# Zero fills on ScalarE, earlier second-tile scores and an earlier w_out load at the start of a fused attention and MLP kernel

## The chip, the cores and the metric

The kernel runs on one core of a Trainium2 chip. The metric is the device time of one execution in microseconds (us); lower is better. TensorE (PE in the profile) multiplies matrices, VectorE (DVE), ScalarE (ACT) and GpSimd (POOL) work element by element, SyncE (SP) issues transfers. GpSimd issues transfers too. All transfers run on the same 16 DMA engines.

## What is computed

Forgetting attention on 8 batches of 8 heads, 576 positions and head size 64, followed by a two-layer MLP with a tanh GELU on the 4608 resulting rows:

```python
scores = scale * q @ k.T                       # per batch and head, 576 x 576
cum    = cumsum(log(clip(f, 1e-4, 1)))         # forget gates
scores = where(causal, -1e9, scores + cum_i - cum_j)
attn   = softmax(scores);  x = attn @ v        # x: 4608 x 512
h      = x @ w_in                              # 512 x 2048
out    = gelu_tanh(h) @ w_out                  # 2048 x 512
```

The kernel never forms the decay matrix. It folds exp(-cum - 64) into the values (tile `vw`) and into a vector `w_bf` that gives the denominators, so that scores only need an exponential and the causal mask.

## The kernel before

**Tiling.** Heads are taken four at a time: 16 quads, two to a batch. A quad's q and k (`q_c`, `k_c`) are loaded with a cast to bf16, and VectorE transposes them into `qT`, `kT` (L197). Scores go to PSUM tiles `ps_s`, of which there are two, each for two heads; ScalarE takes their exponential into `pt` (L268), GpSimd masks the diagonal blocks (L274), TensorE multiplies with `w_bf` for denominators and with `vw` for values (L314 for the first two quads, L328 later), and VectorE normalizes into `xT` (L359). Rows of `xT` are then the input of the MLP, which works on chunks of 512 rows: w_in products (L490 for the first chunk, L373 and L432 later), GELU on ScalarE into `gT`, w_out products (L610 for chunk 0, L540 later).

**Order.** Nothing is scheduled automatically. The whole order is written out as words in tables (`SETUP`, `FRONT` and one table for each later chunk), and `run` issues them one after another; each engine executes its own instructions strictly in that order. The words that matter here:

- `TK.i`, `TQ.i`: transposes of k and q of quad i. `S.i.r`: scores of quad i, part r, with their exponentials; `H.i.r.g` the same for heads 2g and 2g+1 only. For the first two quads, part 0 is the first 256 query rows, parts 1 to 3 the rest.
- `M.i.r`: masks on GpSimd. `D.i.p`: denominators; `V.i.x.p`: values; p is the half (first 256 rows or the rest).
- `CU`, `CW`: the two products that sum the logarithms (L669, L673); `CW` also computes `wT` on ScalarE (L675). `W`: casts of `wT` to `w_bf` on VectorE. `vw`, `VW`: weighted values on VectorE or GpSimd (L214).
- `B.n.c`: n filler matmuls of c columns whose result nobody reads (L239).
- `LP.t`: load of tile t of v of batch 0. `WI.c`, `WO.c`: loads of pieces of w_in (L180, six pieces) and w_out (L184, four pieces), `LQ`, `LK`: of q and k. All of these are issued from GpSimd's queue, in line with its masks. `X@Y` makes the issue of X wait until load Y has landed (`LU.t` is the load `LP.t`).
- `J`, `j`: steps of the first chunk's w_in products for half of its rows (L490). `F.0.n`: n steps of the output product of chunk 0 (L610), sixteen to a block of 128 rows.

A load that GpSimd issues takes one of eight semaphores in turn, so it also waits for the load eight places before it.

**The start.** `setup` issues the loads of f, q and k, clears the tiles whose unused parts are read (on VectorE, L629 to L641), clamps f (L642), takes its logarithm on ScalarE (L643) and transposes it (L648, copied back at L650 and L651). Tile `v_nat` has rows past the 576th position, `vw` a spare slot `LOW`, and `w_bf` the same slot; these are the zero parts that the change touches (L637 to L641).

Of the kernel before, what the change touches and what calls it, by code (L numbers as in the profile page):

```python
# [16 lines left out]
def kernel(  # L17
# [10 lines left out]
    nc = tc.nc  # L28

    B, H, S, D = q.shape  # L30
    BH = B * H
# [35 lines left out]
    LOW, HIGH = NT, NT - 1  # L67

    SETUP = """
        TK.0 LP.0 LP.1  # L70
    """

    FRONT = """
        TQ.0 B.2.256 TR TK.1 SB B.2.128 CU S.0.0 CW B.5.384 B.1.256 TQ.1 W WI.0 WI.1 vw.0.0 LP.2@LQ.0 M.0.0 LP.4 S.0.2 B.3.384 H.1.0.1 H.1.0.0
        vw.1.0 LP.3 WI.2@LU.1 M.1.0.1 D.0.0 M.1.0.0 WI.3 WI.4 WI.5 H.1.1.1 V.0.0.0 H.0.1.1 V.0.1.0 D.1.0 H.0.1.0 V.1.0.0 M.0.1 LQ.2 LK.2 H.1.1.0
        M.1.1 V.1.1.0 H.0.3.0 j.0.0 H.0.3.1 j.0.0 M.0.3 H.1.3.0 j.0.0 vw.0.1 H.1.3.1 j.0.0 M.1.3 VW.1.1 H.1.2.0 D.0.1 H.1.2.1 j.0.0 J.0.1 V.0.1.1
        V.0.0.1 D.1.1 J.0.2 WO.0 WO.1@LU.4 V.1.1.1 V.1.0.1 J.0.3 J.1.0 WO.2@WI.5 WO.3 J.1.1 TQ.2 LK.3 LQ.3 J.1.2 J.1.3 LX.1.0@WO.0 LQ.4 TK.2 X F.0.6
        LK.4 TK.3 S.2.0 M.2.0 LK.5 F.0.9 S.2.2 M.2.2 LX.1.1@WO.2 F.0.10 S.2.1 TQ.3 TQ.4 F.0.10 LV.2.0@LK.5 m.2.1 vw.2 TK.4 S.3.0 f.0.1 CL.2 LQ.5
        VW.3 D.2 f.0.6 S.3.1 m.3.0 F.0.6 V.2.0 S.3.2 TK.5 LK.6 M.3.2 f.0.7 V.2.1 CL.3 S.4.1 m.3.1 LQ.6 F.0.6 TQ.5 H.4.2.1 D.3 H.4.0.1 LQ.7 VW.4
        H.4.0.0 V.3.1 v.3.0 f.0.3 H.4.2.0 CL.4 I.1.0 m.4.1 U.0 LV.2.1@LQ.5 I.1.4 TQ.6 m.4.2.3 I.1.1 I.1.5 U.1 LV.3.0@LQ.7 LV.3.1 m.4.2.2 TK.6 G.0  # L80
        M.4.0 LK.7 LQ.8 LK.8 I.1.2 I.1.3 U.3 K.1.0 K.1.1 K.1.2 I.1.6 I.1.7 G.1.1.2 U.2 X F.1.16 S.5.0 f.1.26 S.5.1 D.4 M.5.0 f.1.16 S.5.2 V.4.0
        m.5.2.3 f.1.10 VW.5 V.4.1 K.1.3 CL.5 m.5.2.2 S.6.0 f.1.10 M.5.1 D.5 f.1.7 S.6.1 V.5.1 f.1.12 V.5.0 T.2 S.6.2 vw.6
    """

    HOMES = {1: 0, 3: 1, 0: 2}
# [41 lines left out]
    def many(n, shape, dtype, name):  # L127
        return [singles.tile(shape, dtype, name=f"{name}{i}") for i in range(n)]
# [6 lines left out]
    v_nat = many(2, [128, NT, H, D], FP32, "v_nat")  # L135
# [3 lines left out]
    vw = many(2, [128, NT + 1, 4, D], BF16, "vw")  # L139
# [10 lines left out]
    w_bf = singles.tile([128, NQ, NT + 1, 4], BF16, name="w_bf")  # L150
# [3 lines left out]
    idle = u4.rearrange("p t n -> p (t n)")[:, 0:512]  # L154
# [34 lines left out]
    def load_one(src, dst, i):  # L189
        b, h0 = i // QPB, 4 * (i % QPB)  # L190
        return nc.gpsimd.dma_start(
            out=dst[i % 2].rearrange("p a d -> p (a d)"),
            in_=src[b, h0:h0 + 4].rearrange("h (p a) d -> (h p) (a d)", p=32))
# [426 lines left out]
    def setup():  # L620
        nc.sync.dma_start(out=f_sb, in_=f.rearrange("b h s -> (b h) s"))
        dmas["LK.0"] = load_one(k, k_c, 0)
        dmas["LQ.0"] = load_one(q, q_c, 0)
        make_identity(nc, ident_f32)
        dmas["LK.1"] = load_one(k, k_c, 1)
        dmas["LQ.1"] = load_one(q, q_c, 1)
        make_upper_triangular(nc, utri_f32, val=1.0, diag=True)

        nc.vector.memset(idle, 0.0)  # L629
        nc.vector.memset(ones_f32, 1.0)  # L630
        nc.vector.memset(logfT, 0.0)
        nc.vector.memset(shift, -64.0)
        nc.vector.memset(wT[64:128, :, HIGH, :], 0.0)
        for t_ in kT:
            nc.vector.memset(t_[:, 0:64], 0.0)
            nc.vector.memset(t_[:, 64 + S:], 0.0)
        for t_ in v_nat:  # L637
            nc.vector.memset(t_[64:128, HIGH, :, :], 0.0)
        for t_ in vw:
            nc.vector.memset(t_[0:64, LOW, :, :], 0.0)  # L640
        nc.vector.memset(w_bf[0:64, :, LOW, :], 0.0)  # L641
        nc.vector.tensor_scalar(f_sb, f_sb, 1e-4, 1.0, op0=ALU.max, op1=ALU.min)  # L642
        nc.scalar.activation(f_sb, f_sb, AF.Ln)  # L643
        idle_ps.append(psO.tile([128, 1024], FP32, name="idle_ps", tag="po"))
        ps_lt = psM.tile([128, NT * BH], FP32, name="ps_lt", tag="m")
        for t in range(NT):
            n = min(128, S - 128 * t)
            nc.tensor.transpose(ps_lt[:n, t * BH:(t + 1) * BH], f_sb[:, 128 * t:128 * t + n], ident_f32)  # L648
        run(SETUP)
        nc.scalar.copy(logfT[:, :HIGH * BH], ps_lt[:, :HIGH * BH])  # L650
        nc.scalar.copy(logfT[0:64, HIGH * BH:], ps_lt[0:64, HIGH * BH:])  # L651

    def triangles(copy):
        for m in causal:
            copy(m, utri_f32)
        copy(causal[1][64:128, 0:64], utri_f32[0:64, 0:64])
# [37 lines left out]
    def cast_w(copy):  # L694
        copy(w_bf[:, :, 0:NT, :], wT)
        copy(w_bf[64:128, :, LOW, :], wT[0:64, :, 0, :])

    def load_values(b, half):
# [2 lines left out]
    ops = {  # L701
        "W": lambda: cast_w(nc.vector.tensor_copy),
        "w": lambda: cast_w(nc.scalar.copy),
        "CU": within_tiles,
        "CW": make_w,
        "SB": lambda: sums_before(nc.gpsimd),
# [38 lines left out]
    def run(table):  # L745

        for word in table.split():
            word, _, gate = word.partition("@")
            name, *args = word.split(".")
            did = ops[name](*map(int, args))  # L750
            did = did if isinstance(did, list) else [did]
            if gate:
                after(did[0], dmas[gate])
            dmas[word.replace("LP", "LU").replace("LX", "LV")] = did[-1]
# [31 lines left out]
    with tc.manual_schedule():  # L786
        setup()
        run(FRONT)
        for c in range(2, NCH):
            play(c)  # L790
        out_part(NCH - 1, CH)
# [30 lines left out]
```

## Time and profile before

| | |
|---|---|
| time, median of 3 runs | 324.67 us (323.61 to 325.16) |
| the profiled execution | 325.03 us, of which the span from first to last instruction is 323.3 us |
| TensorE busy | 310.7 us, 96% of the span |
| VectorE, ScalarE, GpSimd busy | 251.3, 206.9 and 111.4 us |
| chain that ended last | TensorE 89%, DMA 5%, ScalarE 2% |
| of the DMA part, loads of w_in | 3.5% of the span; of q, 1.7% |
| loads of w_in | six, issued from 8.0 to 18.7 us |
| loads of w_out | four, issued from 26.2 to 31.2 us |

How to read it: a busy share is an average over the whole span. The chain is followed back from the last instruction, each step to what released it. Where a step of the chain is a transfer or an engine other than TensorE, TensorE stood still or ran fillers. Idle time of other engines costs nothing in itself.

### The profile page before, as it was taken

How to read it: one execution, taken by the hardware profiler on the slowest of the kernel's cores; microseconds unless marked ns; L12 is line 12 of the kernel's file. 1: busy time of each engine (PE TensorE's matmuls, PEld its weight loads, DVE VectorE, ACT ScalarE, POOL GpSimd, SP SyncE). 2: the span in 40 equal slices, each digit the busy share in tenths (PEclk: the TensorE clock that was granted, in tenths of full speed). 3: DMA queues.
4: the chain of work that ended last, by engine and by line, in shares of the span. 5: the costliest groups of instructions: out<-in, count | busy, mean ns of one | idle time of the engine just before them, and what ended most of it. 6: DMA issues, size and time to landing. Idle time of an engine off the chain costs nothing.

```text
span 323.3 us, 12322 instructions
## 1 busy us (share of the span) xinstructions
PE 310.7 (96%) x5512; PEld 218.4 (68%) x5532; DVE 251.3 (78%) x401; ACT 206.9 (64%) x259; POOL 111.4 (34%) x158
## 2 busy tenths in 40 slices
PE   3898999999999999999999999999999999999995
PEld 1456844544777567776777687667766788788784
DVE  5754338897679899868986898689877969886882
ACT  4696486776757677568657784778666843732830
POOL 8786446650220116700681048303820150000000
PEclk9999999999999999999999999999999999999999
DMA  7999998889302931493129711981120012013013
GB/s 122 235 137 201 208 213 204 173 162 214 93 4 67 183 70 39 97 213 86 36 70 175 152 36 40 171 187 39 34 69 0 14 33 92 1 34 100 0 33 99
DMA packets 47029, 33.45 MB, mean 103 GB/s; under 512 B 29824, under 2 KB 41216, under 8 KB 46976
## 3 DMA queue, kind: packets, MB, share of 16 engines
q0 software_dynamic: 9168, 15.99, 29.0%
q1 hardware_dynamic: 37664, 16.60, 19.5%
q8 instruction: 43, 0.70, 1.0%
q14 instruction: 10, 0.08, 0.1%
q10 hardware_dynamic: 144, 0.07, 0.1%
HBM read 36.85 MB, written 9.44 MB: 143 GB/s over the span
## 4 chain that ended last, share of the span: by engine, by line
PE 89%; DMA 5%; ACT 2%; issue 1%; POOL 1%; DVE 1%; DVEq 0%; POOLq 0%
PE ps_w L540 30%; PE ps_h L373 16%; PE po L328 10%; PE ps_cd L432 8%; PE ps_s L260 8%; PE ps_ab L432 6%; DMA w_in_sb<-in_moe_w_in_dram 3%; PE pso L610 3%; PE ps_h L490 3%; PE ps_h L387 2%; DMA q_c<-in_q_dram 2%; ACT pt L268 1%; PE idle_ps L239 1%; PE ps_o L328 0%; POOL w_in_sb L180 0%
## 5 line engine op out<-in xcount | busy, mean ns | idle before, releaser
L268 ACT ACTIVATE pt<-ps_s 128x1024 bf16<-128x1024 f32 (+2 forms) x100 | 94.0, 988 | 39.0 <-PE ps_s L260 35.2
L274 POOL TENSOR_SCALAR_AFFINE_SELECT pt<-pt 128x512 bf16<-128x512 bf16 (+2 forms) x67 | 39.9, 605 | 107.7 <-ACT pt L268 106.6
L373 PE MATMUL ps_h<-xT,w_in_sb 128*128 128x512 bf16 x228 | 54.5, 379 | 0.6
L540 PEld LDWEIGHTS <-gT 128*32 128x32 bf16 (+1 forms) x1247 | 50.7, 97 | 6.0 <-issue 1.7
L540 PE MATMUL ps_w<-w_out_sb,gT 128*32 128x256 bf16 (+1 forms) x1050 | 47.0, 273 | 0.0
L380 ACT ACTIVATE gT<-ps_h 128x1024 bf16<-128x1024 f32 x30 | 30.6, 1020 | 17.2 <-PE ps_h L373 16.7
L540 PEld LDWEIGHTS <-gsum 128*32 128x32 bf16 (+1 forms) x1256 | 39.3, 97 | 1.4
L373 PEld LDWEIGHTS <-w_in_sb 128*128 128x128 bf16 x240 | 23.4, 98 | 24.3 <-issue 0.4
L260 PE MATMUL ps_s<-qT,kT 32*128 32x64 bf16 (+5 forms) x896 | 37.0, 264 | 1.4 <-DVE qT L197 0.9
L214 POOL TENSOR_TENSOR vw<-v_nat,wT 128x1280 bf16<-128x1280 f32 (+1 forms) x13 | 29.8, 2290 | 4.7 <-DMA v_nat<-in_v_dram 4.3
L540 PE MATMUL ps_w<-usum,gsum 128*32 128x256 bf16 (+1 forms) x832 | 30.6, 273 | 0.0
L260 PEld LDWEIGHTS <-kT 32*128 32x128 bf16 x896 | 16.8, 93 | 19.2 <-issue 13.6
L197 DVE STREAM_TRANSPOSE kT<-k_c 128x576 f32<-128x576 f32 x16 | 19.9, 1243 | 11.1 <-DMA k_c<-in_k_dram 11.1
L441 ACT ACTIVATE gT<-snap 128x512 bf16<-128x512 f32 x45 | 26.1, 625 | 3.0 <-DVE snap L455 2.4
L565 DVE TENSOR_TENSOR o_st<-ps_w,snap 128x512 f32<-128x512 f32 x31 | 21.2, 685 | 8.4 <-PE ps_w L540 7.2
L432 PEld LDWEIGHTS <-w_in_sb 128*128 128x128 bf16 x240 | 23.4, 98 | 6.2 <-issue 1.5
L328 PE MATMUL po<-pt,vw 128*32 128x64 bf16 (+4 forms) x624 | 22.5, 278 | 0.0
L359 DVE TENSOR_TENSOR xT<-po,rb 128x576 bf16<-128x576 f32 x26 | 19.5, 750 | 3.7 <-PE po L328 3.1
L328 PEld LDWEIGHTS <-vw 128*32 128x32 bf16 x672 | 14.5, 97 | 10.2 <-issue 3.7
L432 PEld LDWEIGHTS <-xT 128*128 128x128 bf16 x180 | 17.6, 98 | 5.2
L197 DVE STREAM_TRANSPOSE qT<-q_c 128x576 f32<-128x576 f32 x16 | 19.9, 1244 | 1.1 <-PE ps_s L260 0.7
L432 PE MATMUL ps_cd<-xT 128*128 128x256 bf16 x120 | 18.0, 273 | 0.0
(105 smaller groups left out, 464.9 us busy)
## 6 DMA issues: line engine op xcount, KB each, us to landing
out_dram<-o_st SPq DMA_DIRECT2D x35, 256.0 KB, 2.4
k_c<-in_k_dram POOLq DMA_DIRECT2D x16, 288.0 KB, 5.9
q_c<-in_q_dram POOLq DMA_DIRECT2D x16, 288.0 KB, 6.4
v_nat<-in_v_dram SPq DMA_DIRECT2D x16, 256.0 KB, 6.8
v_nat<-in_v_dram SPq DMA_DIRECT2D x20, 128.0 KB, 5.7
w_out_sb<-in_moe_w_out_dram POOLq DMA_DIRECT2D x4, 512.0 KB, 10.3
v_nat<-in_v_dram POOLq DMA_DIRECT2D x9, 128.0 KB, 5.5
v_nat<-in_v_dram POOLq DMA_DIRECT2D x4, 256.0 KB, 7.5
```

Source lines behind the costliest of these rows:

```text
L197: nc.vector.transpose(out=dst.rearrange("p s c -> p (s c)").bitcast(FP32) .rearrange("p (t a) -> p a t", a=S // 32), in_=src.rearrange("p ...
L214: eng.tensor_mul(vw[i % 2][:, t0:t1], vb[:, t0:t1, h0:h0 + 4, :], wT[:, i, t0:t1, :].unsqueeze(3).to_broadcast([128, t1 - t0, 4, D]))
L260: nc.tensor.matmul(tiles[h // 2][:, h % 2, c0:c0 + nq], key_columns(i, key, h, c), qq[32 * h:32 * h + 32, q0:q0 + nq, c], start=(c == 0 an ...
L268: nc.scalar.activation(p[:, 2 * g:2 * g + 2, off:off + n], t[:, :, 0:n], AF.Exp, scale=scale)
L274: nc.gpsimd.affine_select(out=x, in_=x, compare_op=ALU.is_ge, fill=0.0, base=0, pattern=pattern, channel_multiplier=-1)
L328: nc.tensor.matmul(po[r0:r0 + w.shape[-1], 448 + q0:448 + q0 + nq], w, p[:, h, col:col + nq], start=(key in (0, "low")), stop=(key in ("lo ...
L373: nc.tensor.matmul(ph[:, j, :], w_in_sb[:, dt, 128 * ft:128 * ft + 128], xT[:, dt, CH * c:CH * (c + 1)], start=(dt == 0), stop=(dt == N_DT ...
L380: nc.scalar.activation(gT[:, 2 * pr:2 * pr + 2, :], ph, AF.Gelu_apprx_tanh)
L432: nc.tensor.matmul(ps[:, j], w[:, dt, 128 * j:128 * j + 128], x[:, dt], start=(first and j == 0 and dt == 0), stop=(dt == 1), skip_group_c ...
L441: nc.scalar.activation(gT[:, ft:ft + 2, HC * j:HC * (j + 1)], x, AF.Gelu_apprx_tanh)
L540: nc.tensor.matmul(ps[c0:c0 + width, n, cols[0]:cols[1]], x[:, j, 128 * n + c0:128 * n + c0 + width], w[:, j, cols[0]:cols[1]], start=(fir ...
L565: nc.vector.tensor_add(st, ps, kept[name])
```

## The change

Three things, all in the first 55 us or so. First, the zero fills of `w_bf`, `vw` and `v_nat` leave VectorE and become copies on ScalarE from a tile of zeros (`idle`, which the first memset clears); the two of `vw` stand before the copies of the transposed logarithm, the other three after them. Second, the scores of part 2 of quad 0 come in two halves directly after `CW`, where six fillers stood; three fillers of 256 columns follow them, and three of 384 columns that followed `S.0.2` are dropped. Third, `LP.3` and `WI.2` stand ahead of the scores of quad 1, `WI.2` and `WO.1` no longer name a load to wait for, `WO.0` stands ahead of `M.1.3`. Beside these `D.0.0` moves behind the last w_in issues, `H.0.1.0` ahead of `D.1.0`, and of two words of chunk 0's output product, `F.0.9` and `F.0.10`, the longer one now comes first.

The core of the diff; in the table lines that are left out the words are the same:

```diff
     SETUP = """
-        TK.0 LP.0 LP.1
+        Z.1.2 TK.0 LP.0 LP.1
     """
     FRONT = """
-        TQ.0 B.2.256 TR TK.1 SB B.2.128 CU S.0.0 CW B.5.384 B.1.256 TQ.1 W WI.0 WI.1 vw.0.0 LP.2@LQ.0 M.0.0 LP.4 S.0.2 B.3.384 H.1.0.1 H.1.0.0
-        vw.1.0 LP.3 WI.2@LU.1 M.1.0.1 D.0.0 M.1.0.0 WI.3 WI.4 WI.5 H.1.1.1 V.0.0.0 H.0.1.1 V.0.1.0 D.1.0 H.0.1.0 V.1.0.0 M.0.1 LQ.2 LK.2 H.1.1.0
-        M.1.1 V.1.1.0 H.0.3.0 j.0.0 H.0.3.1 j.0.0 M.0.3 H.1.3.0 j.0.0 vw.0.1 H.1.3.1 j.0.0 M.1.3 VW.1.1 H.1.2.0 D.0.1 H.1.2.1 j.0.0 J.0.1 V.0.1.1
-        V.0.0.1 D.1.1 J.0.2 WO.0 WO.1@LU.4 V.1.1.1 V.1.0.1 J.0.3 J.1.0 WO.2@WI.5 WO.3 J.1.1 TQ.2 LK.3 LQ.3 J.1.2 J.1.3 LX.1.0@WO.0 LQ.4 TK.2 X F.0.6
-        LK.4 TK.3 S.2.0 M.2.0 LK.5 F.0.9 S.2.2 M.2.2 LX.1.1@WO.2 F.0.10 S.2.1 TQ.3 TQ.4 F.0.10 LV.2.0@LK.5 m.2.1 vw.2 TK.4 S.3.0 f.0.1 CL.2 LQ.5
+        TQ.0 B.2.256 TR TK.1 SB Z.0.3.4 B.2.128 CU S.0.0 CW H.0.2.0 H.0.2.1 B.3.256 TQ.1 W WI.0 WI.1 vw.0.0 LP.2@LQ.0 M.0.0 LP.4 LP.3 WI.2 H.1.0.1
+        H.1.0.0 vw.1.0 M.1.0.1 M.1.0.0 WI.3 WI.4 WI.5 D.0.0 H.1.1.1 V.0.0.0 H.0.1.1 V.0.1.0 H.0.1.0 D.1.0 V.1.0.0 M.0.1 LQ.2 LK.2 H.1.1.0 M.1.1
+        V.1.1.0 H.0.3.0 j.0.0 H.0.3.1 j.0.0 M.0.3 H.1.3.0 j.0.0 vw.0.1 H.1.3.1 j.0.0 WO.0 M.1.3 VW.1.1 H.1.2.0 D.0.1 H.1.2.1 j.0.0 J.0.1 V.0.1.1
+        V.0.0.1 D.1.1 J.0.2 WO.1 V.1.1.1 V.1.0.1 J.0.3 J.1.0 WO.2@WI.5 WO.3 J.1.1 TQ.2 LK.3 LQ.3 J.1.2 J.1.3 LX.1.0@WO.0 LQ.4 TK.2 X F.0.6 LK.4 TK.3
+        S.2.0 M.2.0 LK.5 F.0.10 S.2.2 M.2.2 LX.1.1@WO.2 F.0.9 S.2.1 TQ.3 TQ.4 F.0.10 LV.2.0@LK.5 m.2.1 vw.2 TK.4 S.3.0 f.0.1 CL.2 LQ.5 VW.3 D.2
...
     """
...
-        for t_ in v_nat:
-            nc.vector.memset(t_[64:128, HIGH, :, :], 0.0)
-        for t_ in vw:
-            nc.vector.memset(t_[0:64, LOW, :, :], 0.0)
-        nc.vector.memset(w_bf[0:64, :, LOW, :], 0.0)
...
+    def zeros(which):
+
+        todo = [(w_bf[0:64, :, LOW, :], idle[0:64, 0:BH].rearrange("p (i h) -> p i h", h=4))]
+        todo += [(t_[0:64, LOW, :, :], idle[0:64, 0:256].rearrange("p (h d) -> p h d", h=4)) for t_ in vw]
+        todo += [(t_[64:128, HIGH, :, :], idle[64:128, 0:512].rearrange("p (h d) -> p h d", h=H)) for t_ in v_nat]
+        for n in which:
+            nc.scalar.copy(*todo[n])
...
+        "Z": lambda *which: zeros(which),
```

`Z.1.2` clears the two `vw` tiles, `Z.0.3.4` clears `w_bf` and the two `v_nat` tiles.

More of the change, by code (lines that the diff above doesn't have):

```diff
@@ L77 @@
-        V.0.0.1 D.1.1 J.0.2 WO.0 WO.1@LU.4 V.1.1.1 V.1.0.1 J.0.3 J.1.0 WO.2@WI.5 WO.3 J.1.1 TQ.2 LK.3 LQ.3 J.1.2 J.1.3 LX.1.0@WO.0 LQ.4 TK.2 X F.0.6
-        LK.4 TK.3 S.2.0 M.2.0 LK.5 F.0.9 S.2.2 M.2.2 LX.1.1@WO.2 F.0.10 S.2.1 TQ.3 TQ.4 F.0.10 LV.2.0@LK.5 m.2.1 vw.2 TK.4 S.3.0 f.0.1 CL.2 LQ.5
-        VW.3 D.2 f.0.6 S.3.1 m.3.0 F.0.6 V.2.0 S.3.2 TK.5 LK.6 M.3.2 f.0.7 V.2.1 CL.3 S.4.1 m.3.1 LQ.6 F.0.6 TQ.5 H.4.2.1 D.3 H.4.0.1 LQ.7 VW.4
-        H.4.0.0 V.3.1 v.3.0 f.0.3 H.4.2.0 CL.4 I.1.0 m.4.1 U.0 LV.2.1@LQ.5 I.1.4 TQ.6 m.4.2.3 I.1.1 I.1.5 U.1 LV.3.0@LQ.7 LV.3.1 m.4.2.2 TK.6 G.0
@@ L81 @@
-        M.4.0 LK.7 LQ.8 LK.8 I.1.2 I.1.3 U.3 K.1.0 K.1.1 K.1.2 I.1.6 I.1.7 G.1.1.2 U.2 X F.1.16 S.5.0 f.1.26 S.5.1 D.4 M.5.0 f.1.16 S.5.2 V.4.0
-        m.5.2.3 f.1.10 VW.5 V.4.1 K.1.3 CL.5 m.5.2.2 S.6.0 f.1.10 M.5.1 D.5 f.1.7 S.6.1 V.5.1 f.1.12 V.5.0 T.2 S.6.2 vw.6
+        TQ.0 B.2.256 TR TK.1 SB Z.0.3.4 B.2.128 CU S.0.0 CW H.0.2.0 H.0.2.1 B.3.256 TQ.1 W WI.0 WI.1 vw.0.0 LP.2@LQ.0 M.0.0 LP.4 LP.3 WI.2 H.1.0.1
+        H.1.0.0 vw.1.0 M.1.0.1 M.1.0.0 WI.3 WI.4 WI.5 D.0.0 H.1.1.1 V.0.0.0 H.0.1.1 V.0.1.0 H.0.1.0 D.1.0 V.1.0.0 M.0.1 LQ.2 LK.2 H.1.1.0 M.1.1
@@ new lines @@
+        V.1.1.0 H.0.3.0 j.0.0 H.0.3.1 j.0.0 M.0.3 H.1.3.0 j.0.0 vw.0.1 H.1.3.1 j.0.0 WO.0 M.1.3 VW.1.1 H.1.2.0 D.0.1 H.1.2.1 j.0.0 J.0.1 V.0.1.1
+        V.0.0.1 D.1.1 J.0.2 WO.1 V.1.1.1 V.1.0.1 J.0.3 J.1.0 WO.2@WI.5 WO.3 J.1.1 TQ.2 LK.3 LQ.3 J.1.2 J.1.3 LX.1.0@WO.0 LQ.4 TK.2 X F.0.6 LK.4 TK.3
+        S.2.0 M.2.0 LK.5 F.0.10 S.2.2 M.2.2 LX.1.1@WO.2 F.0.9 S.2.1 TQ.3 TQ.4 F.0.10 LV.2.0@LK.5 m.2.1 vw.2 TK.4 S.3.0 f.0.1 CL.2 LQ.5 VW.3 D.2
+        f.0.6 S.3.1 m.3.0 F.0.6 V.2.0 S.3.2 TK.5 LK.6 M.3.2 f.0.7 V.2.1 CL.3 S.4.1 m.3.1 LQ.6 F.0.6 TQ.5 H.4.2.1 D.3 H.4.0.1 LQ.7 VW.4 H.4.0.0 V.3.1
@@ L83 @@
+        v.3.0 f.0.3 H.4.2.0 CL.4 I.1.0 m.4.1 U.0 LV.2.1@LQ.5 I.1.4 TQ.6 m.4.2.3 I.1.1 I.1.5 U.1 LV.3.0@LQ.7 LV.3.1 m.4.2.2 TK.6 G.0 M.4.0 LK.7 LQ.8
+        LK.8 I.1.2 I.1.3 U.3 K.1.0 K.1.1 K.1.2 I.1.6 I.1.7 G.1.1.2 U.2 X F.1.16 S.5.0 f.1.26 S.5.1 D.4 M.5.0 f.1.16 S.5.2 V.4.0 m.5.2.3 f.1.10 VW.5
+        V.4.1 K.1.3 CL.5 m.5.2.2 S.6.0 f.1.10 M.5.1 D.5 f.1.7 S.6.1 V.5.1 f.1.12 V.5.0 T.2 S.6.2 vw.6
     """
```

## The prediction

> **What bounds the kernel now.** I read the page first: TensorE is busy for 96% of the span, so the rest of it, some 13 us, is all there is to win by moving work. The new order touches the start only, so next I read the chain of waits from 0 to 46 us in order of time. Its middle is this (start, length, what):
>
> ```profile
> 2.02 5.38 DMA q_c<-in_q_dram
> 7.43 1.27 DVE qT L197
> 8.74 0.83 PE ps_s L260 x16
> 9.57 1.15 PE cum_ps L673 x2
> 10.72 1.81 PE idle_ps L239 x6
> 12.53 0.71 PE ps_s L260 x8
> 13.24 1.28 ACT pt L268 x2
> 14.53 1.52 ACT pt L268 x2
> 16.12 1.22 POOL pt L274 x2
> 17.34 1.39 POOL w_in_sb L180 x2
> 18.73 11.20 DMA w_in_sb<-in_moe_w_in_dram
> 29.98 1.70 PE ps_h L490 x14
> 32.83 8.85 PE ps_h L490 x80
> ```
>
> To be seen: 1.81 us of filler matmuls stand on the chain, between the log product (L673) and the second-tile scores; those scores let the exponentials of quad 1 run, those the two masks on GpSimd, and only behind the masks are the last three loads of w_in issued (L180). The last load takes 11.20 us and TensorE waits for it. From 29.98 TensorE runs on without a hole to 41.7.
>
> The timeline of ScalarE shows the hole that the fillers make and the room at the start (last bracket: idle time before, and who ended it):
>
> ```profile
> 5.85 0.37 ACT L650 COPY gsum<-ps_lt 128x256 f32<-128x256 f32 x1 [0.94 <-PE ps_lt L648]
> 6.12 0.20 ACT L651 COPY gsum<-ps_lt 64x64 f32<-64x64 f32 x1
> 6.34 1.28 ACT L268 ACT_TABLE_LOAD   x1
> 9.60 1.51 ACT L268 ACTIVATE pt<-ps_s 128x768 bf16<-128x768 f32 x2 [1.98 <-PE ps_s L260]
> 10.99 0.66 ACT L675 ACTIVATE wT<-cum_ps,shift 128x256 f32<-128x256 f32 x2
> 13.22 4.77 ACT L268 ACTIVATE pt<-ps_s 128x640 bf16<-128x640 f32 x6 [1.57 <-PE ps_s L260]
> ```
>
> Last, stretches of half a microsecond (the two last numbers are the share of the 16 DMA engines and GB/s):
>
> ```profile
> 18.00:18.50 0.50, 0.50 (x14) 0.13 (x10) 0.44 (x2) 0.16 (x1) 0.50 (x2) 1.00 0.73 121
> 18.50:19.00 0.50, 0.50 (x16) 0.29 (x8) 0.45 (x1) 0.50 (x1) 0.50 (x2) 1.00 0.80 98
> 22.00:22.50 0.50, 0.50 (x6) 0.27 (x6) 0.00 (x0) 0.47 (x1) 0.50 (x2) 1.00 1.26 147
> 26.00:26.50 0.50, 0.50 (x7) 0.39 (x4) 0.00 (x0) 0.50 (x1) 0.50 (x2) 1.00 1.11 209
> ```
>
> The DMA engines are full nearly throughout (overlapping packets give shares over 1), with a dip just as the last w_in loads are being issued. That dip decides what an earlier issue is worth.
>
> **The change, part by part.** *Zero fills.* VectorE loses five fills: 1.02 us (v_nat, two), 0.31 us (vw, two) and 0.09 us (w_bf). The clamp of f behind them began at 3.77; f was issued at 0.81 and takes 2.7 us, so it can begin at 3.5, 0.27 us earlier. The transposes that follow wait for k and q (idle 1.80 us and 0.18 us before them), so VectorE gives the chain nothing. ScalarE gains five copies. The nearest rows are 0.37 us (128x256), 0.20 us (64x64) and 625 ns (L441, 512 elements wide), so 2 x 0.37 + 0.20 + 2 x 0.63 = 2.2 us. The two of vw lie between the logarithm and the copy of its transposes, where ScalarE idled for 0.94 us. The other three, 1.46 us, push the table load: copies end near 6.05, zeros at 7.5, the load at 8.8; the first exponential starts at 9.60 because of the scores. So 0.8 us of the cover is left and the cost is 0; it would be 1.5 us if the cover were gone.
>
> [...]
>
> *Scores right behind the log product.* The fillers at 10.51 (six) go; the second-tile scores follow in two halves, then three fillers of 256 columns; three of 384 further on go too. The first half needs the first exponential's PSUM (free at 10.3), the second the other one (11.0), and TensorE comes to them at 10.7 and 11.2: no wait. ScalarE then has its work as soon as the weights (L675) are done, at 11.65: 0.64 + 0.64 us, to 12.93. The hole of 1.57 us is gone. What is late next is quad 1: qT of quad 1 is ready at 12.48 (VectorE 11.22 plus 1.26, held by its load, not moved). Its first half takes at most 0.83 us at the early clock, so its exponentials run from 13.35 to 14.87 (2 x 0.76). They ended at 16.05. Net 1.2 us of the 1.57. D.1.0 now stands behind H.0.1.0, which removes waits of 0.25 us (TensorE) and 0.34 us (ScalarE); D.0.0 moves on GpSimd's side only in the text, since GpSimd runs nothing for it. So TensorE reaches the matmul that waits for w_in near 27.8 rather than at 28.97.
>
> *Loads on GpSimd.* Its order barely changes: LP.3 and WI.2 were already behind LP.4 with only scores between, which are not its work, and the dropped wait of WI.2 held nothing (12.37 + 1.60 = 13.97, the issue is at 13.96). What helps is that the masks of quad 1 start at 14.9 instead of 16.12, so WI.3, WI.4 and WI.5 issue 1.2 us earlier, at 16.1 to 18.2. WO.0 moves ahead of the masks M.1.3 and off a place behind VW.1.1: one issue, 0.75 us. It comes at about 21.5, the exponentials for M.1.3 end near 22.4, so the masks and D.1.1 behind them wait for nothing new (0 to 0.75 us, 0 taken, since the issue fits in front). SyncE's queue holds only the load of f before its first store and is not passed. WO.0's 512 KB stand in the queue behind WI.5 and the q and k of quad 2, issued at 20.04 and 20.61; the later w_out loads stay tied to WI.5's landing.
>
> *What the earlier issue is worth.* One bound is 1.2 us: the landing moves with the issue. The other is 0: the queue is full and the transfers end when the bytes are through. Between them stands the dip: against a full share of about 1.1, the stretches at 18.0 and 18.5 lack (0.37 + 0.30) x 0.5 = 0.34 us of DMA time; the dips at 20.0 to 21.5 (0.69, 0.96, 0.91) lack 0.37 us more, but all loads were issued by then. I take 0.5 us, nearer to the dip than to the issue. Everything after 29.98 hangs on this landing and moves with it.
>
> *The swap of F.0.9 and F.0.10.* One step of the output product, some 0.23 us, moves ahead of S.2.2, where TensorE idled for 0.22 us for ScalarE's PSUM (row at 46.10). Worth 0.2 us; bounds 0 and 0.22.
>
> Sum: 0.5 + 0.2 = 0.7 us off. The profiled execution was 325.03 us (span 323.3 and 1.7 around it), 0.36 above the median of 324.67; I count from the median: 324.0 us.
>
> **The rivals.** *A, all of it arrives.* The rate between 22 and 24.5 us is 115 to 147 GB/s at a full share and over 200 from 26 on, as the exponentials end (25.59). If that slow stretch goes with them and ends 1.2 us earlier, 1.2 x (1 - 140/208) = 0.4 us comes on top of the whole issue gain: 1.6 us, with the swap 1.8 us: 322.9 us. The limit is TensorE's own arrival: 29.98 - 27.8 = 2.2 us, with the swap 322.3. Against it: the slow stretch may belong to the loads themselves, and would then only be met earlier.
>
> *B, the transfer does not move.* The issue was hidden by a full queue; only the swap counts: 324.5 us. For it: the shares above 1 up to 17.9 us.
>
> *C, slower: the clock of TensorE comes up late.* In the profile 384-column fillers run at 2.02 us for six at 10.51 and 0.66 us for three at 13.12, so the clock doubled near 13. The change removes the full-array matmuls that stood before that switch and puts half-array scores there. If the switch then waits, each us at the low clock loses about 0.5 us of TensorE's work, which is dense here (11.84 us busy of 12.40 between 13.2 and 25.6). The first 1.7 us lost are hidden by the w_in wait (27.8 to 29.5). To be slower by 0.5% the loss must be 4.1 us, so the clock must stay low to about 21.3. If it stays low until the dense products at 24.8, it loses 5.9 us, of which 2.2 us are covered: 3.7 us, less the swap, 328.2 us. Against it: TensorE has no gap over 0.1 us from 8.74 to 13.3 in the new order either.
>
> [...]
>
> **How the numbers follow.** About 0.5% (1.6 us) is what a measurement of this kernel can tell from no change; the three runs shown spread over 1.55 us. My forecast (0.3 to 1.4 us gained) has 0.45, B 0.16, A or more 0.27, C 0.12. Forecast and B are within 0.5%, so same 0.61, faster 0.27 (323.05 or less), slower 0.12. The range takes in most of A and the scatter above B: 322.5 to 325.4 us.
>
> **What would show it.** In the profile after: ScalarE's 1.57 us of idle gone, exponentials of quad 1 over near 14.9, first exponential still at 9.6 (zeros covered), masks at 14.9, w_in issues from 16.1, and the w_in-bound matmul of 29.98 at about 29.5. If it still starts at 29.9, B holds; at 28.4 or before, A. If second-tile or quad-1 score groups stay slow after 13.5, C. The forecast is wrong, too, if the first exponential slips past 9.8, or if the earlier WO.0 holds up M.1.3.

## The result, and the profile after

The changed kernel is slower: 329.54 us, median of 6 executions (328.68 to 329.95), against 324.65 us for the kernel before, median of 6 (323.61 to 325.16). The ratio is 1.0152, interval 1.0129 to 1.0175. The profiled execution took 329.91 us with a span of 328.2 us, 4.9 us more than the span before. The prediction was 324.0 us with a range up to 325.4: it was wrong, and on the wrong side of no change. One thing is needed to read the runs below: in 4 of 13, 2 of 17 and 4 of 29 executions of the later batches (none of these six) the kernel before itself takes 329.85 to 335.0 us, and ratios are taken over its other executions.

What the prediction looked for on ScalarE is all there. Its timeline after (columns as before; last the idle time and who ended it):

```profile
4.75 0.69 ACT L654 COPY vw<-usum 64x256 bf16<-64x256 bf16 x2
6.16 0.25 ACT L654 COPY w_bf<-usum 64x64 bf16<-64x64 bf16 x1
6.41 1.13 ACT L654 CAST v_nat<-usum 64x512 f32<-64x512 bf16 x2
7.56 1.28 ACT L268 ACT_TABLE_LOAD   x1
9.18 1.51 ACT L268 ACTIVATE pt<-ps_s 128x768 bf16<-128x768 f32 x2 [0.33 <-PE ps_s L260]
11.29 1.27 ACT L268 ACTIVATE pt<-ps_s 128x640 bf16<-128x640 f32 x2
13.26 1.51 ACT L268 ACTIVATE pt<-ps_s 128x768 bf16<-128x768 f32 x2 [0.69 <-PE ps_s L260]
15.19 1.02 ACT L268 ACTIVATE pt<-ps_s 128x1024 bf16<-128x1024 f32 x1 [0.42 <-PE ps_s L260]
```

The copies and the table load end at 8.84, and the first exponential still waits for its scores. The hole of 1.57 us is gone, and quad 1's exponentials are over at 14.77. Then something new shows: from 15.19 on ScalarE waits for scores before every exponential. On GpSimd the masks and the last three loads of w_in come as early as forecast (timeline):

```profile
14.85 1.22 POOL L274 TENSOR_SCALAR_AFFINE_SELECT pt<-pt 128x512 bf16<-128x512 bf16 x2 [0.49 <-ACT pt L268]
16.03 2.14 POOL L180 DMA_DIRECT2D w_in_sb<-in_moe_w_in_dram  x3
```

and the answer for the tile `w_in_sb` gives the last issue and the longest way from issue to landing, that of the last load, so it is there at 27.5 where it was 29.9:

```profile
L180 POOL DMA_DIRECT2D w_in_sb<-in_moe_w_in_dram x6: 704/714/722, 8.0 to 17.5; - x6
...
DMA to landing us min/median/max: 5.5/6.5/10.0
```

But nothing waits for it any more, because TensorE is late. The chain of waits after, from 12 to 47 us:

```profile
12.39 0.84 PE ps_s L260 x10
13.26 0.82 ACT pt L268
14.12 1.03 PE ps_s L260 x8
...
20.88 0.97 PE ps_h L490 x4
21.85 0.75 PE ps_s L260 x8
...
29.43 3.53 PE ps_h L490 x16
...
34.95 1.85 PE ps_h L490 x16
36.81 1.15 PE po_m L314 x40
37.96 8.84 PE ps_h L490 x80
```

The loads of w_in have left the chain and TensorE fills it alone. Sixteen like products (L490) take 3.53 us at 29.43 and 1.85 us at 34.95. The run of 80 products starts at 37.96; before, at 32.83. Row by row, TensorE's timeline before:

```profile
15.39 0.63 PE L260 MATMUL ps_s<-qT,kT 32*128 32x320 bf16 x8
19.86 0.61 PE L490 MATMUL ps_h<-xT,w_in_sb 128*128 128x256 bf16 x4
24.78 1.92 PE L490 MATMUL ps_h<-xT,w_in_sb 128*128 128x256 bf16 x16
26.63 1.22 PE L314 MATMUL po_m<-pt,vw 128*32 128x320 bf16 x40
```

and after, first what stands where the six fillers stood (two-head scores and three shorter fillers), then the like instructions and sixteen more products at the end:

```profile
10.23 1.22 PE L260 MATMUL ps_s<-qT,kT 32*128 32x320 bf16 x8
11.39 0.82 PE L239 MATMUL idle_ps<-usum 128*128 128x256 bf16 x3
15.52 1.03 PE L260 MATMUL ps_s<-qT,kT 32*128 32x320 bf16 x8
20.81 1.03 PE L490 MATMUL ps_h<-xT,w_in_sb 128*128 128x256 bf16 x4
29.37 3.59 PE L490 MATMUL ps_h<-xT,w_in_sb 128*128 128x256 bf16 x16
32.89 1.27 PE L314 MATMUL po_m<-pt,vw 128*32 128x320 bf16 x40
34.89 1.92 PE L490 MATMUL ps_h<-xT,w_in_sb 128*128 128x256 bf16 x16
```

So TensorE ran at half clock until about 33 us. The trace's own record of the granted clock says the same: full from 13.06 us on before, from 33.04 us on after. The record begins with the first rise, so the page's clock line, which is drawn from it, does not show the half clock ahead of it: it has a 9 in every slice, as it had before:

```profile
PEclk9999999999999999999999999999999999999999
```

The balance closes. The stretch from the first denominators (13.37 after, 15.02 before) to the forty value products (32.89 and 26.63) took 19.52 us instead of 11.61, 7.91 us more. It began 1.65 us earlier, and 1.14 us of standing before the run of 80 is gone (26.63 to 32.77 before, 32.89 to 37.89 after). That leaves 5.12 us at the run of 80; 4.9 us arrive at the end of the span; the 0.2 us between are about what the swap in the output product was to save.

### The profile page after: what moved, and what is told of

It reads as the page before. It is cut to its first block, busy times and chain, and to the rows that moved or that the text cites. A ratio compares the mean times of both kernels' runs of the same rounds, so it can differ in the third digit from the quotient of the medians.

```text
span 328.2 us, 12308 instructions
## 1 busy us (share of the span) xinstructions
PE 317.2 (97%) x5506; PEld 219.8 (67%) x5526; DVE 250.1 (76%) x396; ACT 209.3 (64%) x264; POOL 112.0 (34%) x158
## 4 chain that ended last, share of the span: by engine, by line
PE 94%; DMA 2%; issue 1%; DVE 1%; POOL 1%; ACT 0%; POOLq 0%; DVEq 0%
PE ps_w L540 30%; PE ps_h L373 16%; PE ps_s L260 11%; PE po L328 9%; PE ps_cd L432 8%; PE ps_ab L432 6%; PE ps_h L490 6%; PE pso L610 4%; DMA q_c<-in_q_dram 2%; PE ps_h L387 2%; PE po_m L314 2%; PE ps_o L328 0%; DVE qT L197 0%; POOL k_c L191 0%; PE ps_l L540 0%
## 5 line engine op out<-in xcount | busy, mean ns | idle before, releaser
L260 PE MATMUL ps_s<-qT,kT 32*128 32x64 bf16 (+5 forms) x896 | 40.9, 276 | 1.0 <-DVE qT L197 0.7
L260 PEld LDWEIGHTS <-kT 32*128 32x128 bf16 x896 | 17.7, 96 | 21.5 <-issue 15.6
L490 PE MATMUL ps_h<-xT,w_in_sb 128*128 128x256 bf16 x128 | 18.6, 309 | 0.0
```

The lines of the kernel that those rows point to most:

```text
L260: nc.tensor.matmul(tiles[h // 2][:, h % 2, c0:c0 + nq], key_columns(i, key, h, c), qq[32 * h:32 * h + 32, q0:q0 + nq, c], start=(c == 0 an ...
L490: nc.tensor.matmul(ph[:, j // 2, QA * (j % 2):QA * (j % 2) + QA], w_in_sb[:, dt, 128 * ft:128 * ft + 128], xT[:, dt, n0:n0 + QA], start=(d ...
```

## The experiments

The expectations name theories by letters. **F**: the clock doubles only behind enough work on all 128 rows, and the removed fillers supplied it, so that the time comes back with them. **R**: the new order itself costs, whatever the fillers (in experiment 3, the fillers only filled a hole). **G**: only gaps and busy time of TensorE count. **H**: the cause is that the second-tile scores come in halves. Where another letter appears, what it expects stands beside it. Fillers write a PSUM tile that nobody reads, so no kernel below leaves out a part of the computation.

**1. The fillers back in their old place, in the changed kernel.**

```diff
-CW H.0.2.0 H.0.2.1 B.3.256 TQ.1
+CW B.5.384 B.1.256 H.0.2.0 H.0.2.1 B.3.256 TQ.1
```

> The changed kernel with the six fillers of the kernel before (five of 384 columns, one of 256) put back between the log product and the second-tile scores; everything else as changed. [...] Rival R (the new order itself costs the 5 us, on ScalarE or GpSimd): 329 us or more, since the fillers only add work.

Measured: 324.3 us, median of 10 (323.10 to 327.57), ratio 0.9994 (0.9961 to 1.0026). All the rest of the change is in it, and the loss is gone. TensorE's timeline:

```profile
10.34 1.77 PE L239 MATMUL idle_ps<-usum 128*128 128x384 bf16 x6
12.04 0.47 PE L260 MATMUL ps_s<-qT,kT 32*128 32x320 bf16 x8
```

The scores behind the fillers run at full clock (0.47 us; 0.72 before); the record has it from 11.72 us on. R falls. Its chain of waits shows what the earlier issue is worth with the clock up:

```profile
18.05 11.08 DMA w_in_sb<-in_moe_w_in_dram
29.13 0.05 issue
29.18 1.70 PE ps_h L490 x14
```

Issued 0.68 us earlier than before, landed 0.80 us earlier. By the two chains little of the 0.68 is the new order's doing: the first scores began 0.18 us earlier, and the rest comes with the clock, which rose at 11.72 and not at 13.06 us. The run of 80 products starts at 32.03 there, against 32.83 before and 37.96 in the changed kernel, and the span is 322.2 us.

**2. The fillers behind the halves.** The same work for TensorE, placed after the scores.

```diff
-CW H.0.2.0 H.0.2.1 B.3.256 TQ.1
+CW H.0.2.0 H.0.2.1 B.5.384 B.1.256 TQ.1
```

> The changed kernel with those six fillers behind the second-tile scores, in place of the three of 256 columns. Theory F, if half-array scores break the run of whole-array products: the fillers alone are 1.8 us and what follows are halves, so the clock stays low, 328 to 330 us. Rival G (only gaps of TensorE matter): the hole before quad 1's scores (12.2 to 12.4) is closed, there is no gap from 8.3 to 13.7 and the clock doubles by 14: 322.5 to 324.5 us.

Measured: 330.31 us, median of 4 (330.24, 330.39, 330.54, and one of 324.07). In the profile (TensorE's timeline) the six fillers run through at half clock, and what follows stays slow:

```profile
11.41 1.99 PE L239 MATMUL idle_ps<-usum 128*128 128x384 bf16 x6
...
15.05 1.03 PE L260 MATMUL ps_s<-qT,kT 32*128 32x320 bf16 x8 [0.43 <-ACT pt L268]
```

Busy time speaks against G here: TensorE has no gap over 0.1 us from 8.34 to 14.6 us, and the clock stays down. In experiment 1 the same six fillers, right behind the log product, brought it up by 11.72; here scores of two heads stand between. The one execution at 324.07 shows that it is close.

**3. The kernel before, without those fillers.**

```diff
-CW B.5.384 B.1.256 TQ.1
+CW TQ.1
-S.0.2 B.3.384 H.1.0.1
+S.0.2 H.1.0.1
```

> The kernel before without its nine fillers at that place (five of 384 columns, one of 256, three of 384), nothing else. Theory F: the clock doubles only in the first dense products of the MLP, near 30 us, and the time is 328 to 331 us. Rival R (the fillers only filled a hole): 323 to 325 us, because ScalarE's 1.57 us of idle shrinks.

Measured: 329.6 us, median of 4 (329.19 to 330.19), ratio 1.0148 (1.0114 to 1.0182), clock full from 32.99 us. TensorE's timeline has the sixteen products at half clock, as in the changed kernel:

```profile
29.32 3.59 PE L490 MATMUL ps_h<-xT,w_in_sb 128*128 128x256 bf16 x16
```

Taking the fillers away, and nothing else, gives the whole loss. R falls here too.

**4. The changed kernel with the scores whole.**

```diff
-CW H.0.2.0 H.0.2.1 B.3.256 TQ.1
+CW S.0.2 B.3.256 TQ.1
```

> The changed kernel with the second-tile scores of all four heads at once instead of in halves; the three fillers stay. Rival H (the halves, which use half of the rows, keep the clock low): the clock doubles near 13, 322.5 to 324.5 us. Theory F (too little whole-array work, whichever way the scores come): 328 to 330 us.

Measured: 329.75 us, median of 4 (328.54 to 330.38), ratio 1.015 (1.0115 to 1.0185). The split in the order is not what costs: experiment 1 has it too and loses nothing. This run is no test of four heads at once, since in its trace the two groups of `S.0.2` took 1.22 us, as the halves do; each still waited for its PSUM tile. So that half-row products helped to keep the clock down here is not excluded, and F expects it.

**5. Early fillers in the changed kernel.** If only the first rise is missing, whole-row work ahead of everything should supply it. `keep_busy(8)` issues eight fillers of 512 columns before the transposes of the logarithm, `B.2.256` two of 256 before the first scores.

```diff
     def setup():
...
         idle_ps.append(psO.tile([128, 1024], FP32, name="idle_ps", tag="po"))
+        keep_busy(8)
...
-CU S.0.0 CW
+CU B.2.256 S.0.0 CW
```

> The changed kernel with eight fillers of 512 columns ahead of the transposes of the logarithm (TensorE is idle there until 5 us) and two of 256 columns ahead of the first scores, so that whole-array products run with hardly a gap from 1.3 to 10.3 us; the order of the change is kept. [...] Rival T (the switch comes only near 13 us or later whatever ran before): 324 to 330 us.

Measured: 330.24 us, median of 6 (329.65 to 331.29, and one of 322.97). The most telling miss: the clock rose at 6.19 us, which rules out T, and was lost again. TensorE's timeline:

```profile
1.26 3.59 PE L239 MATMUL idle_ps<-usum 128*128 128x512 bf16 x8 [1.26 <-DVE usum L629]
...
8.30 0.52 PE L260 MATMUL ps_s<-qT,kT 32*128 32x256 bf16 x16 [0.94 <-DVE qT L197]
...
12.38 0.55 PE L260 MATMUL ps_s<-qT,kT 32*128 32x256 bf16 x16 [1.05 <-DVE qT L197]
...
13.80 1.04 PE L260 MATMUL ps_s<-qT,kT 32*128 32x320 bf16 x8 [0.53 <-ACT pt L268]
```

The clock did come up (0.52 us at 8.30, against 0.83 us for the same scores before) and was taken back: the eight scores at 13.80 are slow again (1.04 us; 0.63 us for such eight before). The record has it full from 6.19 to 13.02 us, half for 20.48 us, full from 33.50 on. At full clock TensorE finished its early work sooner and then stood waiting for VectorE and ScalarE (0.94 us ahead of 8.30, 0.28, 0.24 and 1.05 us from 9.4 to 12.38, 0.53 us ahead of 13.80); the clock was lost at 13.02, in that thin stretch, and the work behind it, which keeps the clock in the kernel before (full from 13.06 on), did not win it back until 33.50.

**6. The same early fillers in the kernel before.**

```diff
     def setup():
...
+        keep_busy(8)
...
-CU S.0.0 CW
+CU B.2.256 S.0.0 CW
```

> The kernel before with the same early fillers. Theory F: the clock doubles before 9 us in every execution, and the time is that of the kernel before where its clock comes up, 323 to 324.8 us, since its chain through the exponentials, masks and the load of w_in is not bound by TensorE there; the difference to the changed kernel with the same fillers is what the order of the change is worth with the clock out of the way: 1.2 to 2.4 us by the landing of w_in, 0.2 of it the swap. If the order is worth nothing (rival B of the prediction), the two are within 0.5 us.

Measured: two groups, 7 of 12 at 322.5 to 324.5 and 5 at 328.05 to 330.77; the ratio of the first group is 0.9969 (0.9942 to 0.9996). With the clock up from 10.22 us in the traced execution it is a little faster, but 5 of 12 are near 330 us where 2 of 17 of the kernel before in that batch were; these are too few to call it worse. That the clock would be up before 9 us and that none would be near 330 was wrong, and with experiment 5 near 330 too the comparison that should price the new order cannot be made.

**7. Only the two early fillers, in the changed kernel.**

```diff
-CU S.0.0 CW
+CU B.2.256 S.0.0 CW
```

> The changed kernel with only the two fillers of 256 columns ahead of the first scores: whole-array products from 5 to 10.2 us, 5.2 us, then halves. [...] Rival G (gaps matter, not the rows used): no gap from 5 to 12.2, so every execution is near 322.5 us.

Measured: 329.27 us, median of 4 (329.07 to 329.39), ratio 1.0135 (1.0108 to 1.0161). The record: full from 8.73 us for 3.41 us, half for 20.48 us, full from 32.62 on. In the traced execution the clock came early here too and was lost in a thin stretch: TensorE's holes between 8.73 and 12.14, each ended by an engine it waits for, are 0.27, 0.24 and 0.44 us. The other three have a mean granted clock of 1.00, so in them it rose once and late. What G expects fails here too: no execution is near 322.5 us.

**8. Experiment 1 with fillers on half the rows.** Same number, columns and duration of fillers; in all fillers of the kernel only 64 of the 128 rows work.

```diff
-            nc.tensor.matmul(idle_ps[0][:, 0:cols], idle[:, 0:128], idle[:, 0:cols],
+            nc.tensor.matmul(idle_ps[0][:, 0:cols], idle[0:64, 0:128], idle[0:64, 0:cols],
```

> The changed kernel with the six fillers put back between the log product and the second-tile scores, as in the run where that restored the time, but all fillers use 64 of the 128 rows, for the same length of time. Theory F, with the rows that work as what counts: the clock stays low, 328 to 331 us. Rival G (TensorE busy is enough): 322.5 to 324.7 us, as with whole fillers.

Measured: 331.76 us, median of 4 (330.85 to 332.64), ratio 1.0212 (1.0181 to 1.0242), against 324.3 us with whole rows. TensorE's timeline:

```profile
10.06 1.99 PE L239 MATMUL idle_ps<-usum 64*128 64x384 bf16 x6
11.98 0.72 PE L260 MATMUL ps_s<-qT,kT 32*128 32x320 bf16 x8
```

TensorE is as busy as in experiment 1 and the clock stays at half until 32.45 us. This settles F against G: busy time alone did not lift the clock. With 128 rows at work in the fillers it rose at 11.72 us, with 64 at 32.45.

**9. Fillers around whole scores.** With the cause known: the changed kernel with two fillers before the second-tile scores and four behind, the scores whole, to have the clock up and these scores earlier than in experiment 1.

```diff
-CW H.0.2.0 H.0.2.1 B.3.256 TQ.1
+CW B.2.384 S.0.2 B.4.384 TQ.1
```

> The changed kernel with whole-array work kept up to quad 1's scores and little in the way of ScalarE: two fillers of 384 columns behind the log product, then the second-tile scores of all four heads at once (both PSUM tiles are free by then), then four fillers of 384 columns. [...] Rival: the second-tile scores 0.7 us earlier are worth nothing more than in the run with the fillers first: 323.9 to 324.7.

Measured: 323.55 us, median of 12 (322.86 to 324.41), ratio 0.9984 (0.9969 to 1.0000). None of the 12 is near 330, where 4 of 29 executions of the kernel before in that batch stood at 331 us or above. It is the best version found, but its gain is at the edge of what can be measured, and with the kernel before failing at 4 of 29, none of 12 could also be luck. Its chain of waits:

```profile
17.31 10.99 DMA w_in_sb<-in_moe_w_in_dram
28.30 0.05 issue
28.35 1.70 PE ps_h L490 x14
...
31.20 8.84 PE ps_h L490 x80
```

The load is issued 1.42 us earlier than in the profile of before and lands 1.63 us earlier; some 0.6 us of both is this execution's own, since its first q landed that much earlier (6.77 against 7.40).

**10. More fillers.** As 9, with eight fillers behind the scores and two before the first ones, meant to leave no execution near 330 us.

```diff
-CU S.0.0 CW H.0.2.0 H.0.2.1 B.3.256 TQ.1
+CU B.2.256 S.0.0 CW B.2.384 S.0.2 B.8.384 TQ.1
```

> The same with two fillers of 256 columns in TensorE's hole ahead of the first scores, and eight fillers of 384 columns behind the second-tile scores instead of four. Whole-array work then runs from 5 to 13 us at either clock. [...]

Measured: 323.91 us, median of 12 (322.14 to 324.97, and one of 330.82), ratio without that one 0.9993 (0.9974 to 1.0013). One of the 12 is near 330 all the same. The wait for w_in is gone, but its chain shows what is late next:

```profile
30.57 8.84 PE ps_h L490 x80
...
50.79 6.21 DMA v_nat<-in_v_dram
...
57.25 2.34 POOL vw L214
...
59.87 1.79 DVE pt L303
```

The run of 80 starts 0.63 us earlier than in experiment 9, and it brings nothing: twenty us later TensorE waits for a load of v and for the weighted values made from it.

**11. The zero fills alone, in the kernel before.** They move to ScalarE as in the change (words `Z.1.2` and `Z.0.3.4`); the order is otherwise the old one.

```diff
-TK.0 LP.0 LP.1
+Z.1.2 TK.0 LP.0 LP.1
-SB B.2.128
+SB Z.0.3.4 B.2.128
```

> The kernel before with only the zero fills moved to ScalarE. The prediction's step: hidden behind the wait for the first scores, 0 us (323.9 to 325.2), first exponential still waiting for the scores. Rival: the table load behind the copies is late, the first exponential slips and the second-tile scores with it: up to 1.5 us more.

Measured: 324.28 us, median of 10 (323.27 to 325.05), ratio 1.0004 (0.9987 to 1.0020). They cost and bring nothing that can be measured.

## Why the prediction was wrong

*Zero fills, 0 taken:* right. The table load took 1.28 us again, and 0.33 us of cover was left where 0.8 was reckoned with; the first scores came earlier here. Experiment 11 measures the step alone as nil. No idle time to speak of stands around such a load either: before the change the one at 25.61, of 1.28 us, followed 0.02 us behind an exponential, and the next activation 0.02 us behind the load.

*The hole on ScalarE:* right as far as it went. Exponentials of quad 1 over at 14.77 (forecast 14.87), masks at 14.85 (14.9), loads from 16.03 (16.1).

*What the earlier issue is worth, 0.5 us between 0 and 1.2:* the bound was too tight. In the changed kernel the last load landed 2.4 us earlier. The load goes in 16 parts, and the last one alone is far off: before, it ended at 29.93, the fifteenth at 28.37. Its last six packets start at 28.54, as a packet of instructions (27.59 to 28.56) ends; that the two shared a queue is not shown. Elsewhere that tail is shorter, by no pattern found: 0.3 us after the change, 1.1, 0.7 and 1.3 us in experiments 1, 9 and 11. The fifteenth part moved 1.22 us in the changed kernel for an issue 1.27 us earlier. With the clock up it moved 0.30 us for 0.68 (experiment 1), 0.80 for 1.42 (experiment 9), 0.79 for 0.91 (experiment 11), 1.00 for 1.04 (experiment 10) and 1.22 for 1.51 (experiment 6). So between 0.4 and 1.0 of the issue arrives, mostly more than the 0.5 of 1.2 that was taken, and the term left out is the tail, worth up to 1.3 us. That TensorE would wait for this load at all was wrong here for another reason, the next one.

*The swap, 0.2 us:* borne out, by one trace of each kernel. From the start of the run of 80 to the end of the span it is 290.5 us before (323.3 - 32.83), 290.2 in the changed kernel (328.2 - 37.96) and in experiment 1 (322.2 - 32.03), 290.4 in experiment 11 (322.1 - 31.74), which has the old order there. The earlier load of w_out appears in no chain of waits over the first 65 us; it was issued at 24.54 us and not near 21.5, since the masks ahead of it waited for exponentials, and those for scores at half clock.

*The step that failed:* rival C, the late clock, and what was held against it: "TensorE has no gap over 0.1 us from 8.74 to 13.3 in the new order either." That was nearly true (the trace after has one gap of 0.19 us in that stretch), and it is no argument. The prediction saw the clock double near 13, and saw that the change takes the full-array products from before that switch and puts half-array ones there. It then judged by TensorE's busy time, gave C 0.12, and left 0.88 to cases in which the clock comes as before. Its sum of 0.5 + 0.2 us has no term for the clock; the runs put one of 5.1 us there, at the start of the run of 80. Experiment 3 shows that the missing fillers make the whole loss; experiments 1 and 8, alike but for the rows of the fillers, show that busy time alone does not lift the clock (up at 11.72 and at 32.45 us).

The mechanism of C was right and its price low by 1.3 us: 328.2 us forecast, 329.54 measured. (Its threshold of 4.1 us comes to 4.0 by its own terms, 1.6 + 0.7 + 1.7, which changes nothing.) It let the clock come back with the dense products at 24.8. At half clock TensorE reached them only at 29.37, and the clock came up at 33.04, as sixteen of them (3.59 us) were through.

The argument from busy time fails in the changed kernel's own trace: from 12.39 to 29.4 us TensorE had scarcely a gap (0.24 us at 14.12 is the longest) and stayed at half clock. The late clock costs 1.5% here.

## What to carry to other kernels

Matmuls that nobody reads may be what brings TensorE to full speed, as they were here (experiment 3: without them the clock rose at 32.99 us and not at 13.06, and the time was 329.6 us). Before removing one, look in the trace for the place where the pitch of equal matmuls halves, and see which whole-row work stands before it. Read the pitch, not the clock line of the page, and look at how many rows work there, not only at how busy TensorE is: experiments 1 and 8 are equally busy and 7.5 us apart. One kernel can have two times, as in experiment 2 (three executions at 330.24 to 330.54, one at 324.07) and 6 (7 at 322.5 to 324.5, 5 at 328.05 to 330.77); what decides which of them an execution gets was not shown. In experiment 9 six fillers around whole scores had only the faster one in 12 executions, too few to call it cured.

## What the runs showed of the hardware

- **Rows counted for the clock.** Six fillers on 128 rows, after a whole-row product, brought it up at 11.72 us (experiment 1); with all fillers on 64 rows, for about the same duration, it came up at 32.45 (experiment 8): 324.3 against 331.76 us. How much whole-row work it takes, and for how long, no run shows. Between 20.8 and 26.9 us of the changed kernel whole-row products make up some 0.97 us in every 1.72 us, with scores of two heads between them, and the clock stayed at half.
- **The rise came at no fixed time from the start of the kernel, and could be lost.** The kernel before and experiment 1 run the same fillers behind first scores at 8.74 and 8.56 us, and the clock rose at 13.06 and 11.72. In experiment 5 it was full for 6.83 us and then half for 20.48, in experiment 7 full for 3.41 and then half for 20.48. Some kernels fall on either side from one execution to the next (experiments 2, 5, 6 and 10, and the kernel before), and there are two ways to be near 330 us. The mean granted clock of an execution tells them apart, since its record counts half clock only behind the first rise: the changed kernel has 1.00 there with half clock until 33.04 us. It is 1.00 also near 330 us in experiments 2, 3, 4 and 8 and in three of four executions in 7, so there it rose once and late. It is 0.964 to 0.979 in five of six executions in experiment 5, the five near 330 us in 6, one in 7, the one in 10, and all ten of the kernel before. By that mean they ran at half clock for some 14 to 24 us behind the first rise, an estimate from (1 - mean) x 2 x span; the traces of 5 and 7 show the 20.48 us. None of those ten was traced, so where it loses the clock is open.
- **What kept the clock differs from what lifted it.** The mixed work from 13 to 25 us ran at full clock throughout before (full from 13.06) and did not bring it up after (half until 33.04). In experiments 5 and 7 the clock was lost in a stretch with holes: in 7 they are 0.95 us of the 3.41 from 8.73 us. Idle time alone does not decide: the kernel before stands for 1.01 us ahead of 29.98 us, waiting for w_in, and keeps the clock.
